# The order of small loads and of sums of squares in a fused attention and expert kernel

## The chip, the cores and the metric

The kernel runs on one core of a Trainium2 chip. The metric is device time in microseconds (us) of one execution. The engines are named as in the profile: PE is TensorE's products, PEld its weight loads, DVE is VectorE, ACT is ScalarE, POOL is GpSimd, SP is SyncE, whose queue issues nearly all loads.

## What is computed

Attention between channels, then a layer of experts on its result, where each token goes to the one expert with the largest logit:

```python
def _attn_ref(q, k, v, tau):                       # B, N, C = 4, 5056, 256
    qn = q / (np.linalg.norm(q, axis=1, keepdims=True) + 1e-06)
    kn = k / (np.linalg.norm(k, axis=1, keepdims=True) + 1e-06)
    s = kn.transpose(0, 2, 1) @ qn / tau
    s = s - s.max(-1, keepdims=True)
    a = np.exp(s)
    a /= a.sum(-1, keepdims=True) + 1e-09
    return v @ a

def _moe_ref(x, w_gate, w1, w2):                   # E, D, F = 8, 256, 1024; x has 20224 rows
    logits = x @ w_gate
    expert_idx = np.argmax(logits, axis=1)
...
    for e in range(E):
        mask = expert_idx == e
        h = np.maximum(x[mask] @ w1[e], 0.0)
        out[mask] = gate_w[mask, None] * (h @ w2[e])
```

The norms of q and k run over the 5056 tokens, so they are sums of squares by channel.

## The kernel before, in words

The four batches of attention run one after the other, and the experts' work begins as soon as the first batch has routed enough tokens. After that three streams share the engines.

*Blocks of tokens.* 72 blocks of 256 tokens and 18 of 128, in six stages; a stage can begin when a batch of attention is done. `block_load` (lines 683 to 695) makes a block's loads on SP: a register is read from the stage's table (line 687), a transposed load brings the rows `xT` (line 692; three buffers, so it waits until the products of three blocks earlier have read theirs), and a small load brings `mt`, 2 KB with each token's factor and row number (line 694; six buffers, so it waits until the store of six blocks earlier has used its own). `block` (from line 697) does 48 products `hp` in four groups (line 720). ACT takes each group out of PSUM as `ht` (line 728, the eviction) and DVE makes its lower half `ht[:, 1]` (line 729). 48 products `y` follow (line 746), two evictions `o` with the token's factor (line 756) and two indirect stores on POOL (line 759). The products' weights `wp` are copied by DVE (line 708).

*Weights.* `weights` (lines 109 to 156) loads an expert's two matrices, 1 MB each (line 116), takes a Gram matrix for a bound on their size (line 132, scale from line 140), and splits them into two halves of 16 bits on ACT (line 150) and DVE (line 151). This fills the first blocks.

*Attention of the next batch.* Products `sp` of keys and queries (line 219), the softmax, products `px` of values (line 389), their copies `xg` and squares (lines 391 and 393), the conversion `rows` (lines 345 and 346) and the scatter to the experts' places in memory (line 516). Pieces of 512 KB called `fed` come through four buffers, with up to three loads ahead (`feed`, line 476). For the norms `by_channel` (lines 171 to 180) has ACT square a piece stored by channel and sum it along the row: 60 instructions at line 178, 54 of them on a `fed` piece. Their sums are needed only once, when all scores of the batch are there.

What sets the order: the Python code writes the three streams interleaved, in portions whose amounts are laid out per stage, and `look` writes a block's loads two blocks ahead. A scheduler then orders each engine's instructions by when it reckons that their inputs are there; a dependency without a semaphore, as the change adds, only says that one instruction stands behind another in the order. On the chip each engine runs its list strictly in that order, and so does SP's queue: an instruction that waits holds everything behind it.

Of the kernel before, what the change touches and what calls it, by code (L numbers as in the profile page):

```python
# [12 lines left out]
F16 = mybir.dt.float16  # L13
BF16 = mybir.dt.bfloat16
I32 = mybir.dt.int32
AF = mybir.ActivationFunctionType
# [4 lines left out]
P = 128  # L21
B, N, C = 4, 5056, 256
# [4 lines left out]
ROW = 258  # L27
# [37 lines left out]
def attention_then_experts(ctx, tc, qk, v, wt, chs, kc, out):  # L65
    nc = tc.nc
    sync, act, vec, pool, pe = nc.sync, nc.scalar, nc.vector, nc.gpsimd, nc.tensor
# [11 lines left out]
    xs = dram.tile([E * NPAD + BLK, ROW], F32, name="xs")  # L79
# [23 lines left out]
    def cell(n):  # L103
        half = place(n // 2)[:, (n % 2) * 2048 : (n % 2 + 1) * 2048]
        return half.bitcast(F32).rearrange("p (j c) -> p j c", j=2)
# [62 lines left out]

    lengths_of = {b: one.tile([P, 4, 5], F32, tag=f"lengths{b % 2}", name="lengths") for b in range(1, B)}

    def by_channel(b):
        lengths = lengths_of[b]
        for n in range(20):
            if b == 1 and n < 6:
                raw = cell(26 + n).rearrange("p j c -> p (j c)")
            else:
                raw = fed("c", b, n).rearrange("p j c -> p (j c)")
            norm = act.activation(raw, raw, AF.Square, accum_out=lengths[:, n // 5, n % 5 : n % 5 + 1])  # L178
            normed.append(norm.ins.name)
            yield 300  # L180

    def split(raw):
# [296 lines left out]
    def fed(*which):  # L479
        if not loading:  # L480
            feed()
        key, raw = loading.pop(0)
        assert key == which, (key, which)
        return raw
# [9 lines left out]
    behind = [None]  # L494
    issued = [None]
    HERE = mybir.DependencyInfo(mybir.DependencyClass.NoSync, mybir.DependencyReason.DATA)

    def after_dma(ins):
        if issued[0] is not None:
            tc.add_manual_dep(ins.ins, issued[0], HERE, reason="stands between two transfers")  # L500
# [35 lines left out]
    def loaded(stage, ins):  # L536
        raw = ins.ins
        if stage < LAST:
            tc.declare_no_dep(raw, group="pads", reason="behind the tokens")
        for s2 in range(stage + 1, LAST):  # L540
            tc.declare_no_dep(raw, group=f"scatter{s2}", reason="blocks read are full already")
        tc.add_to_no_dep_group("loads", raw)
        for name in written[stage] + (written[stage - 1] if stage == LAST else []):
            tc.add_manual_dep(raw, name, SYNC, reason="the stage's rows")
# [10 lines left out]
    def stored(ins):  # L555
        raw = ins.ins
        tc.declare_no_dep(raw, group="stores", reason="a token has one row")
        tc.add_to_no_dep_group("stores", raw)
# [126 lines left out]
    def block_load(stage, tab, i):  # L685
        nt = P if stage == LAST else BLK
        at = nc.values_load(
            tab[1][0:1, i : i + 1], engines=[ENG.SP], min_val=0, max_val=E * NPAD,
            skip_runtime_bounds_check_because=WHY,
        )  # L690
        xT = work.tile([P, 4, BLK], F16, tag="xT", name="xT", bufs=3)[:, :, 0:nt]
        loaded(stage, sync.dma_start_transpose(out=xT, in_=xs[ds(at, nt), 0:C].bitcast(F16)))
        mt = work.tile([P, 2, 2], F32, tag="mt", name="mt", bufs=6)[:, 0 : nt // P, :]
        loaded(stage, sync.dma_start(out=mt, in_=xs[ds(at, nt), C:ROW].rearrange("(j p) c -> p j c", p=P)))
        return xT, mt

    def block(stage, tab, i, xT, mt):
        nt = P if stage == LAST else BLK
        nj = nt // P
        nf = 512 // nt  # L700
        e = nc.values_load(
            tab[0][0:1, i : i + 1], engines=[ENG.DVE], min_val=0, max_val=i if stage == 0 else E - 1,
            skip_runtime_bounds_check_because=WHY,
        )

        def piece(n):
            t = work.tile([P, 1024], F16, tag="wp", name="wp", bufs=WP)
            vec.tensor_copy(out=t, in_=Wf[:, ds(e * 8192 + n * 1024, 1024)])  # L708
            return t

        hts = []
        for f in range(8):
            if f % 2 == 0:
                wp = piece(f // 2).rearrange("p (d s f) -> p d s f", d=2, s=2)
            if f % nf == 0:
                hp = ps_h.tile([P, nf, nt], F32, tag="hp", name="hp")
            n = 0
            for dc in range(2):
                for wh, xh in ((0, 0), (0, 1), (1, 0)):
                    mm = pe.matmul(  # L720
                        hp[:, f % nf, :], wp[:, dc, wh, (f % 2) * P : (f % 2 + 1) * P], xT[:, 2 * xh + dc, :],
                        start=(n == 0), stop=(n == 5),
                    )
                    n += 1
            behind[0] = mm.ins.name
            if f % nf == nf - 1:
                ht = work.tile([P, 2, nf, nt], F16, tag="ht", name="ht", bufs=4)
                act.activation(ht[:, 0], hp, AF.Relu)  # L728
                halved = vec.scalar_tensor_tensor(  # L729
                    out=ht[:, 1], in0=hp, scalar=0.0, in1=ht[:, 0], op0=ALU.max, op1=ALU.subtract  # L730
                )
                hts.append(ht)
            if f % 2 == 1:
                yield
        fac = tiny.tile([P, 2], F32, name="b_fac")[:, 0:nj]
        by = vec.tensor_scalar(out=fac, in0=mt[:, :, 0], scalar1=fe[:, ds(e, 1)], scalar2=None, op0=ALU.mult)
        tc.add_manual_dep(by.ins, halved.ins.name, HERE, reason="the block's rows are here")
        ys = ps_y.tile([P, 2, C], F32, tag="y", name="y")
        wps = []
        for j in range(nj):  # L740
            for n, (hh, wh, f) in enumerate(
                [(0, wh, f) for f in range(8) for wh in range(2)] + [(1, 0, f) for f in range(8)]
            ):
                if j == 0 and n < 16 and n % 4 == 0:
                    wps.append(piece(4 + f // 2).rearrange("p (f s d) -> p f s d", f=2, s=2))
                mm = pe.matmul(  # L746
                    ys[:, j, :], hts[f // nf][:, hh, f % nf, j * P : (j + 1) * P], wps[f // 2][:, f % 2, wh, :],
                    start=(n == 0), stop=(n == 23),
                )
                if (j * 24 + n + 1) % (6 * nj) == 0 and j * 24 + n + 1 < 24 * nj:  # L750
                    behind[0] = mm.ins.name
                    yield
        behind[0] = mm.ins.name
        for j in range(nj):
            o = work.tile([P, C], F32, tag="o", name="o", bufs=2)
            act.activation(o, ys[:, j, :], AF.Copy, scale=fac[:, j : j + 1])  # L756
            gap = pool.memset(idle, 0.0)  # L757
            after_dma(gap)
            ins = pool.indirect_dma_start(  # L759
                out=out[:, :], out_offset=bass.IndirectOffsetOnAxis(ap=mt.bitcast(I32)[:, j, 1:2], axis=0),  # L760
                in_=o, in_offset=None, bounds_check=NT - 1, oob_is_err=False,
            )
            tc.add_manual_dep(ins.ins, gap.ins.name, HERE, reason="behind the pause")
            issued[0] = ins.ins.name
            stored(ins)
        yield
# [46 lines left out]
    rest = work.tile([P, K_N - K_TRI], F32, tag="junk", name="rest", bufs=1)  # L813
# [41 lines left out]
    while len(ahead_of) > G - CUT:  # L855
        fetch()
    norms = by_channel(1)
    take(norms, 6)
    while ahead_of:
# [18 lines left out]
    def look(n, now=True):  # L878
        if n < len(stages) and n not in ahead and stages[n][0] in tables and (now or stages[n][1] > 1):
            ahead[n] = block_load(stages[n][0], tables[stages[n][0]], stages[n][1])  # L880
# [84 lines left out]
    def sides():  # L965
# [3 lines left out]
        yield 0  # L969

    norms_of = {b: by_channel(b) for b in range(2, B)}
    parts = [42 * 1000 + HALF * CHUNK + 10 * 300, 5000 + X_ALL + HALF * CHUNK + 10 * 300]
    parts += [5000 + X_ALL + nch * CHUNK + 20 * 300, 5000 + X_ALL]
# [28 lines left out]
    with tc.If(nc.values_load(  # L1002
        tables[LAST][2][0:1, 0:1], min_val=0, max_val=REST_MOST, skip_runtime_bounds_check_because=WHY
    ) > REST_USUAL):
        more = range(REST_USUAL, REST_MOST)
        loads = {i: block_load(LAST, tables[LAST], i) for i in more}
        for i in more:
            run(block(LAST, tables[LAST], i, *loads[i]))
# [36 lines left out]
```

## Time and profile before

| | |
|---|---|
| median of 3 runs | 1209.59 us (1205.8 to 1214.18) |
| the profiled execution | 1208.84 us, its span in the trace 1207.0 |
| busy: PE, PEld | 1162.8, 1024.9 us |
| busy: DVE, ACT, POOL | 805.6, 619.7, 462.0 us |
| DMA | 177.38 MB, mean 147 GB/s |

The page names for each engine how long it was busy, for groups of instructions what ended the idle time before them, and for stretches of time the granted clock of TensorE and the busy share of the 16 DMA engines. "SPq" is SP's own queue, in which a time is that of issuing a DMA and not of its transfer.

### The profile page before, as it was taken

To read this page: it belongs to the slowest core of one execution; us is meant where nothing else is said; L and a number is where in the kernel's file an instruction comes from. 1 tells how busy PE (TensorE), PEld (TensorE's weight loads), DVE (VectorE), ACT (ScalarE), POOL (GpSimd) and SP (SyncE) were. 2 spreads that over 40 slices of the span, in tenths; PEclk is the share of its full clock that TensorE was granted. 3 is DMA by queue.
4 is the path that set the end of the run, shared out by engine and by line. 5 is a ranking of instruction groups with operands and counts; after the bars stand their busy time and mean duration, and the time that the engine had idled before them with its cause. 6 is when DMAs were issued, how large, how long until landed. Compare 5 with 4: busy or idle time off the path is not lost. (4 is left out here: it accounts for less than half of the span.)

```text
span 1207.0 us, 28339 instructions
## 1 busy us (share of the span) xinstructions
PE 1162.8 (96%) x10194; PEld 1024.9 (85%) x10194; DVE 805.6 (67%) x2122; ACT 619.7 (51%) x1385; POOL 462.0 (38%) x724
## 2 busy tenths in 40 slices
PE   9998899899989999999999999999999999999998
PEld 7777688688878888888888988999878888889997
DVE  5575587767685776666677666767675555556886
ACT  6576377678736665555543555555423333333332
POOL 0066712117771343343345235454462222222222
PEclk9999899999999999999999999999999999999999
DMA  9968989768735555655534232322142122211221
GB/s 377 410 256 291 344 327 269 250 191 244 225 97 146 153 163 159 156 155 163 159 104 104 62 98 84 93 72 75 49 127 53 45 54 54 50 45 45 54 46 26
DMA packets 153488, 177.38 MB, mean 147 GB/s; under 512 B 116604, under 2 KB 118017, under 8 KB 151424
## 3 DMA queue, kind: packets, MB, share of 16 engines
q1 hardware_dynamic: 137952, 133.94, 38.1%
q0 software_dynamic: 15392, 41.60, 9.3%
q8 instruction: 81, 1.33, 0.5%
q14 instruction: 63, 0.52, 0.2%
HBM read 111.49 MB, written 43.29 MB: 128 GB/s over the span
## 5 line engine op out<-in xcount | busy, mean ns | idle before, releaser
L746 PE MATMUL y<-wp,ht 128*128 128x256 f16 x3888 | 457.1, 273 | 15.3 <-ACT ht L728 9.7
L720 PE MATMUL hp<-xT,wp 128*128 128x256 f16 (+1 forms) x4320 | 452.0, 262 | 5.8 <-DVE ht L729 3.8
L746 PEld LDWEIGHTS <-ht 128*128 128x128 f16 x3888 | 372.4, 98 | 71.3 <-ACT ht L728 18.3
L720 PEld LDWEIGHTS <-wp 128*128 128x128 f16 x4320 | 383.0, 98 | 52.1 <-DVE ht L729 4.5
L708 DVE COPY wp<-W 128x1024 f16 (+1 forms) x720 | 291.9, 439 | 181.7 <-PE y L746 138.4
L759 POOL DMA_INDIRECT out<-o,mt x162 | 180.1, 1112 | 480.1 <-ACT o L756 456.8
L728 ACT ACTIVATE ht<-hp 128x512 f16<-128x512 f32 x324 | 191.3, 593 | 160.9 <-PE hp L720 159.0
L729 DVE SCALAR_TENSOR_TENSOR ht<-hp,ht 128x512 f16<-128x512 f32 x324 | 222.3, 687 | 62.6 <-ACT ht L728 61.3
L516 POOL DMA_INDIRECT xs<-rows,r_si x160 | 180.9, 1130 | 141.6 <-ACT rows L345 58.8
L756 ACT ACTIVATE o<-y,b_fac 128x256 f32<-128x256 f32 x162 | 68.9, 468 | 230.8 <-PE y L746 224.5
L506 POOL TENSOR_SCALAR rows<-kt 128x1 int32<-128x1 f32 x160 | 45.5, 284 | 117.2 <-PE sp L219 81.2
L391 ACT COPY xg<-px 128x264 f32<-128x264 f32 x160 | 57.9, 368 | 61.3 <-PE px L389 40.3
L345 ACT ACTIVATE rows<-xg,x_sc 128x256 f16<-128x256 f32 x160 | 71.1, 498 | 25.7 <-issue 8.6
L178 ACT ACTIVATE fed<-fed 128x1024 f32<-128x1024 f32 x54 | 57.0, 1055 | 50.5 <-DMA fed<-in_by_channel 50.4
L346 DVE SCALAR_TENSOR_TENSOR rows<-xg,x_sc,rows 128x256 f16<-128x256 f32 x160 | 71.2, 480 | 15.4 <-ACT rows L345 15.0
L187 DVE TENSOR_TENSOR lo<-fed,hi 128x1024 fp32r<-128x1024 f32 x50 | 61.9, 1239 | 29.1 <-ACT hi L185 29.1
L389 PE MATMUL px<-a_h,hi 128*128 128x264 f32 x240 | 73.3, 308 | 1.5 <-ACT xg L391 0.8
L389 PE MATMUL px<-a_h,lo 128*128 128x264 f32 x240 | 67.3, 287 | 1.2 <-DVE lo L187 1.1
L393 ACT ACTIVATE xjunk<-xg 128x256 bf16<-128x256 f32 x160 | 66.6, 416 | 2.9
L389 PE MATMUL px<-a_l,hi 128*128 128x264 f32 x240 | 67.7, 285 | 0.0
L185 ACT CAST hi<-fed 128x1024 fp32r<-128x1024 f32 x50 | 52.0, 1040 | 17.4 <-DVE c_sf L648 12.3
L389 PEld LDWEIGHTS px<-a_h,hi 128*128 128x128 f32 x240 | 45.2, 189 | 5.8 <-ACT hi L185 2.1
(161 smaller groups left out, 971.5 us busy)
## 6 DMA issues: line engine op xcount, KB each, us to landing
fed<-in_by_channel SPq DMA_DIRECT2D x54, 512.0 KB, 4.3
fed<-in_qk SPq DMA_DIRECT2D x40, 512.0 KB, 4.5
W<-in_w SPq DMA_DIRECT2D x15, 1024.0 KB, 12.9
fed<-in_v SPq DMA_DIRECT2D x30, 512.0 KB, 4.4
raw<-in_qk SPq DMA_DIRECT2D x20, 512.0 KB, 10.1
W<-in_qk SPq DMA_DIRECT2D x20, 512.0 KB, 10.2
W<-in_v SPq DMA_DIRECT2D x10, 512.0 KB, 10.2
W<-in_by_channel SPq DMA_DIRECT2D x6, 512.0 KB
```

Source lines behind the costliest of these rows:

```text
L345: act.activation(r16[:, t, 0:C], x, AF.Copy, scale=by)
L346: vec.scalar_tensor_tensor(out=r16[:, t, C : 2 * C], in0=x, scalar=by, in1=r16[:, t, 0:C], op0=ALU.mult, op1=ALU.subtract)
L389: mm = pe.matmul(px, hl[vh][:, c, ts], ah[:, c, :], start=(n == 0), stop=(n == 5))
L393: act.activation(junk, xg[:, t, 0:C], AF.Square, accum_out=ss[:, h * T + t : h * T + t + 1])
L516: ins = pool.indirect_dma_start(out=xs[:, :], out_offset=bass.IndirectOffsetOnAxis(ap=slot[:n], axis=0), in_=row[:n], in_offset=None)
L708: vec.tensor_copy(out=t, in_=Wf[:, ds(e * 8192 + n * 1024, 1024)])
L720: mm = pe.matmul(hp[:, f % nf, :], wp[:, dc, wh, (f % 2) * P : (f % 2 + 1) * P], xT[:, 2 * xh + dc, :], start=(n == 0), stop=(n == 5),)
L728: act.activation(ht[:, 0], hp, AF.Relu)
L729: halved = vec.scalar_tensor_tensor(out=ht[:, 1], in0=hp, scalar=0.0, in1=ht[:, 0], op0=ALU.max, op1=ALU.subtract)
L746: mm = pe.matmul(ys[:, j, :], hts[f // nf][:, hh, f % nf, j * P : (j + 1) * P], wps[f // 2][:, f % 2, wh, :], start=(n == 0), stop=(n == 23),)
L756: act.activation(o, ys[:, j, :], AF.Copy, scale=fac[:, j : j + 1])
L759: ins = pool.indirect_dma_start(out=out[:, :], out_offset=bass.IndirectOffsetOnAxis(ap=mt.bitcast(I32)[:, j, 1:2], axis=0), in_=o, in_offs ...
```

## The change

A block's small load gets a dependency, for order alone, on its own transposed load. Each square of `by_channel` gets one on the eviction `ht` that was written last before it in the source, whichever block that belongs to. No instruction is added or taken away. Behind the change line numbers are higher: 178 is 184, 692 is 699, 694 is 702, 728 is 738, 756 is 766, 476 is 483.

```diff
@@ -168,6 +168,12 @@
 
     lengths_of = {b: one.tile([P, 4, 5], F32, tag=f"lengths{b % 2}", name="lengths") for b in range(1, B)}
 
+    evicted = []
+
+    def in_turn(ins):
+        if evicted:
+            tc.add_manual_dep(ins.ins, evicted[-1], HERE, reason="behind what the products wait for")
+
     def by_channel(b):
         lengths = lengths_of[b]
         for n in range(20):
@@ -177,6 +183,7 @@
                 raw = fed("c", b, n).rearrange("p j c -> p (j c)")
             norm = act.activation(raw, raw, AF.Square, accum_out=lengths[:, n // 5, n % 5 : n % 5 + 1])
             normed.append(norm.ins.name)
+            in_turn(norm)
             yield 300
 
     def split(raw):
@@ -689,9 +696,12 @@
             skip_runtime_bounds_check_because=WHY,
         )
         xT = work.tile([P, 4, BLK], F16, tag="xT", name="xT", bufs=3)[:, :, 0:nt]
-        loaded(stage, sync.dma_start_transpose(out=xT, in_=xs[ds(at, nt), 0:C].bitcast(F16)))
+        turned = sync.dma_start_transpose(out=xT, in_=xs[ds(at, nt), 0:C].bitcast(F16))
+        loaded(stage, turned)
         mt = work.tile([P, 2, 2], F32, tag="mt", name="mt", bufs=6)[:, 0 : nt // P, :]
-        loaded(stage, sync.dma_start(out=mt, in_=xs[ds(at, nt), C:ROW].rearrange("(j p) c -> p j c", p=P)))
+        rest = sync.dma_start(out=mt, in_=xs[ds(at, nt), C:ROW].rearrange("(j p) c -> p j c", p=P))
+        tc.add_manual_dep(rest.ins, turned.ins.name, HERE, reason="behind its rows")
+        loaded(stage, rest)
         return xT, mt
 
     def block(stage, tab, i, xT, mt):
@@ -725,7 +735,7 @@
             behind[0] = mm.ins.name
             if f % nf == nf - 1:
                 ht = work.tile([P, 2, nf, nt], F16, tag="ht", name="ht", bufs=4)
-                act.activation(ht[:, 0], hp, AF.Relu)
+                evicted.append(act.activation(ht[:, 0], hp, AF.Relu).ins.name)
                 halved = vec.scalar_tensor_tensor(
                     out=ht[:, 1], in0=hp, scalar=0.0, in1=ht[:, 0], op0=ALU.max, op1=ALU.subtract
                 )
```

The first place is ACT in the first block after the first batch of attention. `ht_1252`, `ht_1326`, `ht_1346` and `ht_1372` are the evictions of block 0, `ht_1492` to `ht_1551` three of block 1, `o_1453` and `o_1459` block 0's output; `W_82` with `scales_83` is the split of weights. Before:

```order
L728 ACTIVATE ht_1252<-hp_1239 128x512
L178 ACTIVATE fed_1307,lengths_84<-fed_1307 128x1024
L178 ACTIVATE fed_1309,lengths_84<-fed_1309 128x1024
L728 ACTIVATE ht_1326<-hp_1313 128x512
L150 ACTIVATE W_82<-W_82,scales_83 128x4x256
L728 ACTIVATE ht_1346<-hp_1333 128x512
L150 ACTIVATE W_82<-W_82,scales_83 128x4x256 x2
L728 ACTIVATE ht_1372<-hp_1359 128x512
L150 ACTIVATE W_82<-W_82,scales_83 128x4x256
L756 ACTIVATE o_1453<-y_1379,b_fac_1377 128x256
```

Now, from block 0's second eviction on:

```order
L738 ACTIVATE ht_1326<-hp_1313 128x512
L150 ACTIVATE W_82<-W_82,scales_83 128x4x256
L738 ACTIVATE ht_1346<-hp_1333 128x512
L150 ACTIVATE W_82<-W_82,scales_83 128x4x256 x2
L738 ACTIVATE ht_1372<-hp_1359 128x512
L766 ACTIVATE o_1453<-y_1379,b_fac_1377 128x256
L766 ACTIVATE o_1459<-y_1379,b_fac_1377 128x256
L738 ACTIVATE ht_1492<-hp_1479 128x512
L738 ACTIVATE ht_1529<-hp_1516 128x512
L738 ACTIVATE ht_1551<-hp_1538 128x512
L184 ACTIVATE fed_1307,lengths_84<-fed_1307 128x1024
L184 ACTIVATE fed_1309,lengths_84<-fed_1309 128x1024
```

Both squares have moved from behind block 0's first eviction to behind block 1's third.

The second place is SP's queue in the same stretch: the loads of block 2 (`xT_1498` and `mt_1500`), of an expert's two matrices (`W_82`) and of pieces (`fed`). Before:

```order
L476 DMA fed_1309<-in_by_channel 128x1024
L476 DMA fed_1355<-in_qk 128x1024
L687 TENSOR_LOAD c_tb_815
L694 ISA
L694 DMA mt_1500<-xs_81 128x2x2
L109 TENSOR_LOAD perm_132
L116 ISA
L116 DMA W_82<-in_w 128x2048
L116 ISA
L116 DMA W_82<-in_w 128x2048
L692 ISA
L692 DMA_TRANSPOSE xT_1498<-xs_81 128x4x256
```

Now:

```order
L483 DMA fed_1309<-in_by_channel 128x1024
L483 DMA fed_1355<-in_qk 128x1024
L483 DMA fed_1625<-in_qk 128x1024
L694 TENSOR_LOAD c_tb_815
L699 ISA
L699 DMA_TRANSPOSE xT_1498<-xs_81 128x4x256
L702 ISA
L702 DMA mt_1500<-xs_81 128x2x2
L109 TENSOR_LOAD perm_132
L116 ISA
L116 DMA W_82<-in_w 128x2048
L116 ISA
```

The transposed load has moved ahead of the small load and of the weights, and one piece, `fed_1625`, has moved ahead of all of them.

The third place is ACT some 350 us later: `ht_6481`, `ht_6509` and, behind the copies of attention, `ht_6569` and `ht_6589` are evictions of block 20, `ht_6915` to `ht_6979` are those of block 22. Before:

```order
L728 ACTIVATE ht_6481<-hp_6468 128x512
L728 ACTIVATE ht_6509<-hp_6496 128x512
L178 ACTIVATE fed_6734,lengths_86<-fed_6734 128x1024
L391 COPY xg_6529<-px_6530 128x264
L391 COPY xg_6529<-px_6540 128x264
L393 ACTIVATE xjunk_6538,x_ss_6166<-xg_6529 128x256
L393 ACTIVATE xjunk_6548,x_ss_6166<-xg_6529 128x256
L728 ACTIVATE ht_6569<-hp_6556 128x512
L728 ACTIVATE ht_6589<-hp_6576 128x512
L178 ACTIVATE fed_6827,lengths_86<-fed_6827 128x1024
```

Now, where the two squares stand:

```order
L738 ACTIVATE ht_6787<-hp_6774 128x512
L352 ACTIVATE rows_7407<-xg_6529,x_sc_6167 128x256 x2
L192 CAST hi_6879<-fed_6631 128x1024
L766 ACTIVATE o_6867<-y_6792,b_fac_6790 128x256
L766 ACTIVATE o_6873<-y_6792,b_fac_6790 128x256
L192 CAST hi_7060<-fed_6895 128x1024
L738 ACTIVATE ht_6915<-hp_6902 128x512
L738 ACTIVATE ht_6940<-hp_6927 128x512
L738 ACTIVATE ht_6958<-hp_6945 128x512
L184 ACTIVATE fed_6734,lengths_86<-fed_6734 128x1024
L738 ACTIVATE ht_6979<-hp_6966 128x512
L184 ACTIVATE fed_6827,lengths_86<-fed_6827 128x1024
```

The square of `fed_6734` has moved from behind block 20's second eviction to behind block 22's third, and that of `fed_6827` to behind its fourth.

## Rows read from the trace of the kernel before

**Rows 1.** The page's first part: busy time of each engine, its share, instructions.

```profile
PE 1162.8 (96%) x10194; PEld 1024.9 (85%) x10194; DVE 805.6 (67%) x2122; ACT 619.7 (51%) x1385; POOL 462.0 (38%) x724
```

**Rows 2.** 100-us stretches: length; busy PE, PEld, DVE, ACT, POOL; clock, DMA share, GB/s.

```profile
100.00:200.00 100.00, 94.40 (x751) 80.62 (x749) 73.86 (x208) 65.85 (x128) 46.96 (x75) 0.97 0.90 307
200.00:300.00 100.00, 92.19 (x741) 79.17 (x739) 70.77 (x190) 78.19 (x185) 36.82 (x51) 1.00 0.76 232
```

**Rows 3.** Waits by engine: waiting line, releaser, us in total, times, longest.

```profile
ACT fed L178 <- DMA fed<-in_by_channel: 50.4, 31, 5.1
...
PE y L746 <- ACT ht L728: 9.7, 8, 1.9
```

**Rows 4.** Timeline of ACT, first block: start, us, line, tiles, idle before and releaser.

```profile
133.71 1.06 ACT L178 ACTIVATE fed<-fed 128x1024 f32<-128x1024 f32 x1 [5.09 <-DMA fed<-in_by_channel]
...
136.41 1.06 ACT L178 ACTIVATE fed<-fed 128x1024 f32<-128x1024 f32 x1 [1.55 <-DMA fed<-in_by_channel]
...
137.46 0.58 ACT L728 ACTIVATE ht<-hp 128x512 f16<-128x512 f32 x1
```

**Rows 5.** Timeline of PE in the same stretch.

```profile
138.09 0.61 PE L746 MATMUL y<-wp,ht 128*128 128x256 f16 x4 [1.69 <-ACT ht L728]
139.62 1.03 PE L746 MATMUL y<-wp,ht 128*128 128x256 f16 x4 [0.91 <-ACT ht L728]
142.30 2.32 PE L746 MATMUL y<-wp,ht 128*128 128x256 f16 x10 [1.65 <-ACT ht L728]
```

**Rows 6.** That stretch: all of PE; then line 746 alone, with PEld (columns as rows 2).

```profile
135.80:148.60 12.80, 8.55 (x53) 0.73 1.05 337
...
135.80:148.60 12.80, 7.68 (x48) 5.18 (x47) 0.73 1.05 337
```

**Rows 7.** The chain that ended last, a later block: start, us, what.

```profile
706.72 5.24 PE y L746 x48
```

**Rows 8.** Stretches of 2 us, columns as in rows 2.

```profile
140.00:142.00 2.00, 0.65 (x4) 0.15 (x1) 2.00 (x3) 1.99 (x3) 1.93 (x2) 0.50 1.19 390
...
168.00:170.00 2.00, 2.00 (x36) 1.97 (x33) 2.00 (x5) 2.00 (x5) 1.21 (x1) 1.00 0.11 35
```

**Rows 9.** Timeline of SP's own queue (DMA issues), first block.

```profile
128.64 1.24 SPq L116 DMA_DIRECT2D W<-in_w  x2
136.00 4.44 SPq L692 DMA_TRANSPOSE xT<-xs  x1
```

**Rows 10.** Timeline of PE, 200 to 260 us.

```profile
211.91 1.48 PE L720 MATMUL hp<-xT,wp 128*128 128x256 f16 x12 [1.96 <-DVE ht L729]
...
229.05 1.48 PE L720 MATMUL hp<-xT,wp 128*128 128x256 f16 x12 [0.87 <-DVE ht L729]
...
232.16 2.62 PE L746 MATMUL y<-wp,ht 128*128 128x256 f16 x22 [0.76 <-ACT ht L728]
...
254.74 0.39 PE L389 MATMUL px<-a_h,hi 128*128 128x264 f32 x1 [0.84 <-ACT xg L391]
```

**Rows 11.** Timeline of PE and ACT, 370 to 554 us.

```profile
377.20 1.48 PE L746 MATMUL y<-wp,ht 128*128 128x256 f16 x12 [1.44 <-ACT ht L728]
...
488.83 1.06 ACT L178 ACTIVATE fed<-fed 128x1024 f32<-128x1024 f32 x1 [3.08 <-DMA fed<-in_by_channel]
...
492.01 4.22 PE L746 MATMUL y<-wp,ht 128*128 128x256 f16 x35 [1.94 <-ACT ht L728]
...
519.64 2.31 PE L746 MATMUL y<-wp,ht 128*128 128x256 f16 x18 [0.54 <-ACT ht L728]
...
550.86 2.36 PE L746 MATMUL y<-wp,ht 128*128 128x256 f16 x20 [0.74 <-ACT ht L728]
```

**Rows 12.** Waits of SP's own queue: line, releaser, us in total, times, longest.

```profile
SPq L694 <- DMA out<-o,mt: 383.6, 66, 11.8
...
SPq L692 <- PE hp L720: 67.4, 20, 10.9
...
SPq L476 <- ACT fed L178: 69.6, 37, 11.5
```

## Prediction

> **What bounds the kernel now.** I read the page's engine shares first. TensorE (PE) is busy for 1162.8 of 1207.0 us, the next engine, VectorE (DVE), for 805.6, ScalarE (ACT) for 619.7 [rows 1]. So PE's products set the time, and a change that adds and removes no instruction can win back only part of the 44.2 us in which PE stands idle, and what PE loses while it counts as busy. The windows of 100 us come second: PE is at 94.40 us of 100 in the second and 92.19 in the third, where ACT is at 78.19 [rows 2]. The list of waits comes third. PE waits 9.7 us, 8 times, for the eviction `ht` of line 728 that ACT makes; ACT itself waits 50.4 us, 31 times, for the load of a piece that it is about to square [rows 3]. ACT works in order, so an eviction queued behind such a square waits for that load too. The question is how often that reaches PE, and the timelines answer it stretch by stretch.
>
> **The change part by part: the opening.** In the first block ACT stands idle 5.09 us for one piece, squares it from 133.71, waits 1.55 us for the next, squares that from 136.41, and only at 137.46 starts the eviction that follows [rows 4]. PE, in the same stretch, waits for evictions three times, 1.69, 0.91 and 1.65 us, together 4.25 [rows 5]. That is not all of it. The 48 `y` products of this block lie between 135.80 and 148.60, 12.80 us in which PE is busy 8.55, of which 7.68 are theirs, so 0.87 is other work [rows 6]; in a later block 48 such products take 5.24 [rows 7]. The stretch thus loses 12.80 - 5.24 - 0.87 = 6.7 us. The 2.4 us beyond the idle time have a visible cause: behind the idle time the granted clock is 0.50 from 140 to 142, the lower of its two levels (1.2 GHz), with a mean of 0.73 over the stretch [rows 6, 8].
>
> The Trainium skill (Perfetto Trace Analysis, Identifying the Most-Contended Engine) says that matmul busy time judges poorly how near a kernel is to its limit. Its reading and the idle time differ here, 6.7 against 4.25, and the products' own length decides for the larger.
>
> The change puts both squares behind the second block's third eviction, about one block later, so none of the first block's four evictions has a load to wait for any more. The scale factors of the next expert's weights, which ACT now splits between those evictions, do not hang on these loads. I take the whole 6.7 as removed.
>
> Something comes in exchange on SyncE's queue (SP). Before, two weight loads of 1 MB each are issued at 128.64, ahead of the third block's transposed load, which is issued at 136.00 and takes 4.44 us to issue [rows 9]. Now the block's small load follows its transposed load, and the weights follow both. The transposed load waits for a buffer that the first block's last `hp` product frees, so it can't go much before 136. The weights are issued 136.00 - 128.64 = 7.4 us later at best and 11.8 if the transposed load takes 4.44 again; one load of 512 KB moves up into the gap. DMA runs at 390 GB/s here, and only from 168 to 170 does its share fall to 0.11 [rows 8]. The backlog that ended at 168 will end later, by an estimated 5 us (7.4 to 11.8, less what is still in flight at 128.64 and the load that moved up). Up to about 170 that is hidden by products which have their pieces already; behind it the pieces of keys come late. Bounds: 0, since no row has PE waiting for such a load, to 5.5. I take 1.5, near the zero, for that reason. Opening: -6.7 + 1.5 = -5.2.
>
> **200 to 232 us.** PE waits 1.96, 0.87 and 0.76, sum 3.59, behind evictions that had squares ahead of them on ACT [rows 10]. But ACT has its fullest 100 us here, 78.19 busy [rows 2], no square goes away, and one put behind an eviction stands ahead of the next thing. Bounds: -3.6 to +2.5 (two squares of 1.06, with their read-outs, ahead of something that PE wants). I take a third of the gain, -1.2.
>
> **254 to 554 us.** Single waits on ACT with a square shortly ahead: 0.84 at 254.74 [rows 10], then 1.44, 1.94, 0.54 and 0.74 [rows 11]; sum 5.50. At 488.83 the pattern is plain: ACT waits 3.08 us for a piece, squares it, copies products of attention out, and the eviction that PE waits for until 492.01 stands behind all that [rows 11]. In the new order this square comes some two blocks later, behind an eviction for which its piece has long landed, so this wait goes, and the others likewise. The clock did not fall there, so the idle time is the whole price. What is late next is the operand that DVE prepares. Bounds: all of it to half of it, if in the other half something else of ACT takes the square's place. I take -5.5.
>
> **The later small load.** SP waits 383.6 us, 66 times, at line 694 for a store of six blocks earlier [rows 12]. This sounds like the largest item and is worth nothing by itself: SP computes nothing, and no product waits for the small load, which is used only at the end of the block's first half. Its effect is indirect: loads of pieces stand behind it. Behind the transposed load, the small load's buffer has long been free, and that wait should all but vanish; the pieces are then held by the transposed load, which waits for PE (67.4 us, 20 times, before [rows 12]). One holder replaces another, with the pieces about as early. What hides the difference is the queue of four piece buffers with three loads ahead.
>
> **New waits.** Each square now keeps its buffer longer, up to two blocks. SP already waits 69.6 us, 37 times, for squares to free buffers [rows 12]; that grows, and behind it stand the pieces of keys and values that PE needs. Bounds: 0 (the three loads ahead cover it) to 5 us, a few waits like the ones above. I take +2.
>
> **Sum.** -5.2 - 1.2 - 5.5 + 2.0 = -9.9. The profiled execution took 1208.84 us, 1.8 more than its span, which gives 1198.9; the median of the runs is 0.75 higher and would give 1199.7. I say 1199. From the bounds, the best sum is -6.7 - 3.6 - 5.5 = -15.8 (1193), the worst -1.2 + 2.5 - 2.7 + 5 = +3.6 (1212).
>
> **The rivals.**
>
> All of it comes back: the three loads ahead cover the longer holds and the weights aren't missed. For: no row shows PE waiting for a piece's load. Against: ACT's load in the third 100 us. 1193.
>
> Half of it: ACT's total work is unchanged, so where an eviction moves ahead, the copy of an attention product or the split of a piece falls behind. Then only the opening's idle time, less the late loads (-4.25 + 1.5), and half of the later waits (-2.7) come back, with 1 to 2 us of new ones: -4, 1205. That the change does little at all ends here too; that it does nothing is excluded by the order of instructions, in which the squares do move.
>
> Slower: SP stops at the transposed load, and all loads behind it stop. The rows have this holder 20 times, 3.4 us each on average and 10.9 at most [rows 12]. It decides if a piece that PE needs stands behind it with less than 3.4 us to spare. Place one is the opening, where the weights' 11.8 us come through in full instead of 1.5: -6.7 + 11.8 = +5.1. Place two is the stretch of pieces up to 620 us: five holds that come through at 3.4 make +17, against -6.7 won there. Sum +15, 1224. Against it: the holder stood there before, and no piece was late by it.
>
> On that rival the Trainium skill (DMA: Bandwidth & Descriptors, Anatomy of one DMA) says that DMA engines don't wait on semaphores: any wait happens on the issuing sequencer before dispatch. The trace agrees, as each of these waits is SP's own [rows 12]; by this rule alone every load behind the transposed one would be late by its wait, and the time would be that rival's.
>
> **How the numbers follow.** Forecast (1196 to 1203) 0.37, all of it (1189 to 1196) 0.28, half (1203 to 1212) 0.20, slower (1212 to 1226) 0.15. About 1% is what a measurement of this kernel can tell from no change, here 12.1 us: below 1197.5 counts as faster. That is all of "all" and a third of the forecast's case, 0.28 + 0.12 = 0.40. Slower is what of the last case lies above 1221.7, with a little for what I haven't thought of: 0.12. The rest is 0.48. The range 1190 to 1212 leaves out the last case and a sliver at the bottom, under 0.2.
>
> **What would show it.** In the profile after: the first block's four evictions follow their products at once, PE has no wait for `ht` between 136 and 143, and the clock stays at 1.00 there; ACT's wait for pieces to square falls from 50.4 us to under 20; SP's wait at the small load falls from 383.6 to near nothing, and its wait at the transposed load for `hp` grows; the single waits of 254 to 554 are gone, and PE in the third 100 us is little better than 92.19. Wrong it would be if PE waits for a piece's load, for the split of a piece or for weights behind 165 us, with more than 3 us in sum (the late loads), or if PE idles in the third 100 us as long as before or longer (ACT as the bound there).

## The result and the profile after

The changed kernel takes 1197.95 us (median of 6 runs, 1196.92 to 1198.99) against 1210.38 before (6 runs, 1204.81 to 1214.18). The ratio on record is 0.9909, 95% interval 0.989 to 0.9928; the two medians alone give 0.9897, which lies inside it. The profiled execution has a span of 1196.4 us against 1207.0, so it is 10.6 us shorter.

The engine shares of the page and three of the 100-us windows, which answer to [rows 1, 2]; the last row is the fourth window of the kernel before:

```profile
PE 1162.0 (97%) x10194; PEld 1026.0 (86%) x10194; DVE 807.1 (67%) x2122; ACT 618.4 (52%) x1385; POOL 458.8 (38%) x724
```

```profile
100.00:200.00 100.00, 96.90 (x788) 83.21 (x787) 78.33 (x216) 69.29 (x132) 46.29 (x76) 1.00 0.94 320
200.00:300.00 100.00, 95.13 (x757) 80.92 (x755) 70.62 (x191) 77.41 (x191) 43.71 (x60) 1.00 0.79 237
300.00:400.00 100.00, 92.47 (x745) 80.43 (x746) 71.94 (x216) 58.37 (x151) 47.65 (x78) 0.97 0.49 142
```

```profile
300.00:400.00 100.00, 92.37 (x766) 80.33 (x764) 72.32 (x222) 60.09 (x158) 54.85 (x85) 1.00 0.54 155
```

PE is busy for 0.8 us less than before and idle for 34.4 us instead of 44.2, so the gain is idle time. The second and third 100 us are fuller, by 2.5 and 2.9 us. The fourth has 92.47 busy where before it had 92.37 at a clock of 1.00, and now the clock's mean is 0.97. Something new has come there.

The list of waits, which answers to [rows 3]:

```profile
ACT fed L184 <- DMA fed<-in_by_channel: 13.7, 8, 3.2
...
PEld L756 <- ACT ht L738: 7.2, 28, 1.0
...
PE px L396 <- ACT hi L192: 5.5, 2, 3.2
```

ACT's wait for pieces that it squares has fallen from 50.4 to 13.7 us. Of the waits for the eviction `ht`, only short ones are left: 7.2 us of PE's weight loads, 1.0 at most, and 1.7 us of its products, 0.8 at most (9.7 before). New are two waits for the split of a piece, `hi`.

The waits of SP's own queue, which answer to [rows 12]:

```profile
SPq L699 <- PE hp L730: 332.6, 62, 11.1
SPq L483 <- ACT fed L184: 78.6, 32, 9.2
...
SPq L699 <- PE px L396: 62.1, 10, 10.4
```

The wait at the small load, 383.6 us before, is down to 0.9 in sum and too far down the list to stand here. The wait at the transposed load for `hp` products has grown from 67.4 to 332.6, that for `px` products from 11.5 to 62.1. As time in which SP stands still, the one has replaced the other.

*The opening.* ACT after (columns as in rows 4), then PE (as in rows 5), with one 2-us window of all engines (as in rows 8), then SP (as in rows 9):

```profile
131.91 1.15 ACT L150 ACTIVATE W<-W,scales 128x1024 f16<-128x1024 f32 x1 [3.16 <-DVE scales L87]
132.97 0.58 ACT L738 ACTIVATE ht<-hp 128x512 f16<-128x512 f32 x1
...
134.48 0.58 ACT L738 ACTIVATE ht<-hp 128x512 f16<-128x512 f32 x1
...
137.26 0.58 ACT L738 ACTIVATE ht<-hp 128x512 f16<-128x512 f32 x1
...
149.02 1.05 ACT L184 ACTIVATE fed<-fed 128x1024 f32<-128x1024 f32 x1
```

```profile
135.92 1.47 PE L756 MATMUL y<-wp,ht 128*128 128x256 f16 x12
...
137.40 3.17 PE L226 MATMUL sp<-fed 128*128 128x256 f32 x12
140.40 4.09 PE L756 MATMUL y<-wp,ht 128*128 128x256 f16 x36
...
159.17 3.01 PE L756 MATMUL y<-wp,ht 128*128 128x256 f16 x26 [1.18 <-DVE ht L739]
```

```profile
140.00:142.00 2.00, 2.00 (x18) 1.70 (x17) 1.79 (x11) 0.00 (x0) 1.78 (x3) 1.00 1.09 275
```

```profile
126.04 9.10 SPq L483 DMA_DIRECT2D fed<-in_qk  x2
136.12 1.39 SPq L699 DMA_TRANSPOSE xT<-xs  x1
...
138.95 4.83 SPq L116 DMA_DIRECT2D W<-in_w  x7
```

All four evictions of the first block (132.97 to 137.26, and one earlier) run beside the splits of weights, and the squares come at 149.02. PE goes from block 0's `y` through twelve products of scores and the rest of `y` without a stop, and the clock stays at 1.00 where it was 0.50. PE's own order has changed with it: before, two products of scores stood among block 0's `y`, now twelve do. The transposed load is issued at 136.12 and the weights at 138.95, 10.3 us later than before.

Where the gain was made and lost, by blocks: reading the start of each block's last `y` product from both traces, each counted from its kernel's first `y` product, the changed kernel is ahead by 5.1 us at the end of block 1, 4.2 at block 3, 6.2 at block 5, 8.5 at block 6, 8.2 at block 7, only 2.3 at block 9, 4.3 at blocks 12 to 19, and 10.6 from block 28 on. About 1 us of the 8.5 is not won: eight `px` products of block 6 are done in block 7 now. So 5.9 us are lost between blocks 7 and 9. That is the fourth 100 us. ACT there, then PE, then three windows of PE alone (busy, clock, DMA share, GB/s):

```profile
298.99 1.06 ACT L184 ACTIVATE fed<-fed 128x1024 f32<-128x1024 f32 x1 [3.22 <-DMA fed<-in_by_channel]
...
300.05 0.64 ACT L398 COPY xg<-px 128x264 f32<-128x264 f32 x2
...
300.98 1.04 ACT L192 CAST hi<-fed 128x1024 fp32r<-128x1024 f32 x1
```

```profile
302.08 0.44 PE L396 MATMUL px<-a_h,hi 128*128 128x264 f32 x1 [3.24 <-ACT hi L192]
...
324.81 0.39 PE L396 MATMUL px<-a_h,hi 128*128 128x264 f32 x1 [2.25 <-ACT hi L192]
```

```profile
302.00:304.00 2.00, 1.92 (x9) 0.57 0.61 213
304.00:306.00 2.00, 2.00 (x10) 0.58 0.82 229
306.00:308.00 2.00, 2.00 (x15) 1.00 0.13 41
```

A square waits on ACT until 298.99 for its load. The copies `xg` and the split `hi` stand behind it, and PE waits 3.24 us for the split; then the clock is near a half for four microseconds. The same happens at 324.81, behind which the clock is 0.54 and 0.60 in the windows from 326 to 330.

### The profile page after: what moved, and what is told of

Read it like the earlier page. It is cut to its first block, busy times and chain, and to the rows that moved or that the text cites. A ratio compares the mean times of both kernels' runs of the same rounds, so it can differ in the third digit from the quotient of the medians.

```text
span 1196.4 us, 28325 instructions
## 1 busy us (share of the span) xinstructions
PE 1162.0 (97%) x10194; PEld 1026.0 (86%) x10194; DVE 807.1 (67%) x2122; ACT 618.4 (52%) x1385; POOL 458.8 (38%) x724
## 5 line engine op out<-in xcount | busy, mean ns | idle before, releaser
L730 PEld LDWEIGHTS <-wp 128*128 128x128 f16 x4320 | 383.6, 98 | 46.4 <-issue 2.6
L184 ACT ACTIVATE fed<-fed 128x1024 f32<-128x1024 f32 x54 | 56.7, 1050 | 13.7 <-DMA fed<-in_by_channel 13.7
## 6 DMA issues: line engine op xcount, KB each, us to landing
W<-in_w SPq DMA_DIRECT2D x15, 1024.0 KB, 10.6
```

Of the source, the lines that this page charges most:

```text
L730: mm = pe.matmul(hp[:, f % nf, :], wp[:, dc, wh, (f % 2) * P : (f % 2 + 1) * P], xT[:, 2 * xh + dc, :], start=(n == 0), stop=(n == 5),)
```

## The experiments

All times are medians, with the ratio to the kernel before in the same batch. My theory was that the place of the squares carries the change and that the small load by itself is worth nothing; the rival was that the small load carries it, since loads of pieces queue behind it.

**The squares alone.** The tie of the small load is left out.

```diff
-        tc.add_manual_dep(rest.ins, turned.ins.name, HERE, reason="behind its rows")
```

> Squares behind evictions, the small load free as before. If the place of the squares carries the change (mine): the opening's three waits for ht and the single waits at 254 to 554 us are gone as in the full change, 8 to 11 us under before, about 1200. If the small load carries it, because pieces come earlier once SP no longer stops at it: at most 3 us under before, about 1208. SP's wait at the small load is then some 380 us again under both.

Measured: 1210.95 us against 1211.84, ratio 0.9989 (0.9972 to 1.0007), no difference that can be told from none. That is within what I wrote for the rival and far from my own 8 to 11 us. The opening's wait is gone (4.9 us ahead at the end of block 0, counted as above), and then all of it and more is lost: 2.1 us behind at block 1, 7.9 at block 4. PE, SP and ACT of this kernel, two windows of PE, and SP's wait at the small load between 209 and 219 us:

```profile
156.49 2.93 PE L226 MATMUL sp<-fed 128*128 128x256 f32 x6 [5.37 <-DMA fed<-in_qk]
...
223.62 1.03 PE L755 MATMUL y<-wp,ht 128*128 128x256 f16 x4 [4.59 <-ACT ht L737]
```

```profile
130.25 0.33 SPq L116 DMA_DIRECT2D W<-in_w  x1
137.42 3.40 SPq L699 DMA_TRANSPOSE xT<-xs  x1
141.42 0.89 SPq L116 DMA_DIRECT2D W<-in_w  x2
142.36 0.64 SPq L483 DMA_DIRECT2D fed<-in_qk  x1
...
217.59 0.40 SPq L702 DMA_DIRECT2D mt<-xs  x1
218.08 0.89 SPq L483 DMA_DIRECT2D fed<-in_by_channel  x2
```

```profile
221.93 1.06 ACT L184 ACTIVATE fed<-fed 128x1024 f32<-128x1024 f32 x1 [4.89 <-DMA fed<-in_by_channel]
...
222.99 0.58 ACT L737 ACTIVATE ht<-hp 128x512 f16<-128x512 f32 x1
```

```profile
154.00:156.00 2.00, 0.00 (x0) 0.52 1.05 438
...
158.00:160.00 2.00, 2.00 (x7) 0.50 0.98 410
```

```profile
SPq L702 <- DMA out<-o,mt: 7.7, 1, 7.7
```

At 156.49 PE has waited 5.37 us for a piece of queries and keys. SP issued its load at 142.36, behind weights issued at 130.25 and 141.42 and a transposed load that took 3.40 us; in the full change this piece was issued by 135, ahead of all of them. No wait at a small load is part of that: between 126 and 143 SP waits 6.7 us at the transposed load and not at the small one, so in the opening the tie acts by the order in which SP's loads are put. At 221.93 ACT has waited 4.89 us for a piece to square, whose load was issued at 218.08, right behind a small load that went at 217.59 after SP had waited 7.7 us at it for a store; SP's wait at small loads is 360.7 us again here. This place is the wait of SP that the rival meant. The eviction at 222.99 stands behind this square, and PE waits 4.59 us for it. So a square behind an eviction still blocks the next eviction if its own load is late.

**The small load alone.** The squares are free.

```diff
-            in_turn(norm)
```

> The small load behind its transposed load, the squares free as before. Mine: the two squares of the opening stand ahead of the second eviction again, PE waits some 4 us there and its clock falls, and the time is within 3 us of before, about 1209. If the small load carries the change: 8 us or more under before, about 1201, with ACT's wait for pieces to square well under 50 us.

Measured: 1205.16 us, ratio 0.9943 (0.9923 to 0.9963): 6.7 us under before, more than I allowed and less than the rival asked. The squares do stand ahead of the second eviction again, and ACT waits for pieces nearly as long as before:

```profile
ACT fed L184 <- DMA fed<-in_by_channel: 44.7, 31, 4.4
```

```profile
140.29 0.61 PE L755 MATMUL y<-wp,ht 128*128 128x256 f16 x4 [0.91 <-ACT ht L737]
142.85 1.27 PE L755 MATMUL y<-wp,ht 128*128 128x256 f16 x10 [1.95 <-DVE W L151]
```

```profile
140.00:150.00 10.00, 7.70 (x66) 6.36 (x67) 9.83 (x31) 6.50 (x10) 8.48 (x12) 1.00 1.02 327
```

The opening's waits are there, in other sizes: with an idle time of 0.43 at 138.77 they make 3.29 us, against 4.25 before, and the clock stayed at 1.00 in this execution. At the end of block 0 it is 3.0 us ahead of the kernel before, so about 2 of these are the clock's; whether the small load brings that or the single execution did is not shown. Neither theory is right as it stood: by the ratios the parts give 0.1% and 0.6%, together 0.91% and, in the last batch below, 1.05%.

**The squares also behind the split.**

```diff
+        if cast:
+            tc.add_manual_dep(ins.ins, cast[-1], HERE, reason="behind the split of the piece before it")
...
-        act.copy(out=hi, in_=raw)
+        cast.append(act.copy(out=hi, in_=raw).ins.name)
```

> The full change, and each square also behind the last split of a piece that precedes it in the source. In the changed kernel PE waits 3.24 us at 302 and 2.25 at 325 for such a split, each with the clock at a half behind it, and on ACT a square that waits for its load stands ahead of the split. Mine: that square is the cause, both waits shrink to under 1 us, and the time is 4 to 6 us under the changed kernel, about 1193. Rival: the split's own piece or its buffer is late (a load held at the transposed load), the waits stay, and the time is that of the changed kernel, 1198, within 1.5 us.

Measured: 1191.23 us, ratio 0.9832 (0.9808 to 0.9856), clear of the changed kernel's interval and the fastest of all. By the ratios (0.9909 and 0.9895 for the changed kernel in its two batches) that is 8 to 9 us under the changed kernel, more than the 4 to 6 I expected. ACT near 300 us, its wait for pieces, and two 100-us windows:

```profile
297.61 1.05 ACT L194 CAST hi<-fed 128x1024 fp32r<-128x1024 f32 x1
...
299.88 1.06 ACT L186 ACTIVATE fed<-fed 128x1024 f32<-128x1024 f32 x1 [0.81 <-DMA fed<-in_by_channel]
```

```profile
ACT fed L186 <- DMA fed<-in_by_channel: 7.9, 8, 1.7
```

```profile
200.00:300.00 100.00, 95.98 (x766) 82.30 (x763) 73.50 (x196) 79.82 (x198) 42.64 (x59) 1.00 0.78 241
300.00:400.00 100.00, 95.51 (x809) 84.09 (x808) 75.00 (x222) 60.00 (x154) 50.62 (x81) 1.00 0.53 159
```

The split now runs at 297.61 and the square behind it, still with a wait of 0.81 us for its load, which now holds up nothing that PE needs. The two waits of 3.24 and 2.25 us are gone, the clock is 1.00, and the fourth 100 us has 95.51 us of PE instead of 92.47. Counted by blocks, this kernel is 1.3 us ahead of the changed one at block 7 and 9.5 at block 9, so these two places are worth 8.2. The order on ACT was the cause there and not the split's own piece.

**The tie of the squares in the opening only.**

```diff
-            in_turn(norm)
+            if b == 1 and n < 8:
+                in_turn(norm)
```

> Only the first two squares of the blocks' time are tied behind an eviction, the later 52 are free; the small load as in the change. Mine: the opening's part alone, 4 to 5 us under before, about 1205.5, with the waits at 254 to 554 us back. If the opening's gain is given back later (products only arrive earlier at the next wait): within 2 us of before. If the later squares cost as much as they give: about 1198, as the full change.

Measured: 1203.51 us, ratio 0.9929 (0.9906 to 0.9952), 8.3 us under before. The number is nearest to my case, but I had set it without the 6.7 us that the small load brings alone. The later waits are back, in part:

```profile
228.07 2.19 PE L757 MATMUL y<-wp,ht 128*128 128x256 f16 x18 [1.57 <-ACT ht L739]
```

Against the full change in its two batches (0.9909 and 0.9895) the later squares' tie is worth 0.2 to 0.3%, and the intervals overlap. Against the small load alone (0.9943) the tie of the two opening squares adds 0.14%, and these intervals overlap, too: that the opening's squares win anything on top of the small load is not shown by the times.

After these four I took the theory to be: the squares' place wins only if loads of pieces don't stand behind weights or behind SP's wait at a small load. The next two runs test that, with the changed kernel again beside them.

**The small load tied in the first stage only.**

```diff
-        tc.add_manual_dep(rest.ins, turned.ins.name, HERE, reason="behind its rows")
+        if stage == 0:
+            tc.add_manual_dep(rest.ins, turned.ins.name, HERE, reason="behind its rows")
```

> The full change, but the small load is tied to its transposed load only in the first stage, 5 blocks; from block 5 on it is free. If the small load matters only through the opening (there the tie lets a piece of keys go ahead of the weights): the time of the full change, 1198, within 2 us. If later small loads matter too, because pieces queue behind SP's wait at them: up to the 4.6 us that PE lost at 224 us with the squares alone, and more, so 1203 or above.

Measured: 1206.15 us, ratio 0.9946 (0.9926 to 0.9966). The opening keeps its gain (5.1 us ahead at the end of block 1), and the wait that the squares alone had at 224 is back:

```profile
216.41 1.03 PE L757 MATMUL y<-wp,ht 128*128 128x256 f16 x4 [4.63 <-ACT ht L739]
```

From block 3 to block 4 the kernel falls back by 5.7 us. Just ahead SP waits 8.1 us at the small load that goes at 210.33, and the loads of pieces stand behind it. So later small loads matter too.

**Squares behind eviction and split, small load free.** The third experiment without the tie of the small load.

> Squares behind eviction and split, the small load free everywhere. If the small load's tie is needed for what the squares' place gives (my theory after the first four runs): the opening loses some 7 us again to the piece of keys behind the weights, PE waits some 5 us for it at 156 us, and the time is 1199 or above, against 1191 with the tie. Rival: the tie only helped because squares stood ahead of splits; then 1191 to 1193 without it.

Measured: 1202.94 us, ratio 0.9925 (0.9903 to 0.9946), against 1191.23 with the tie.

```profile
155.42 2.93 PE L228 MATMUL sp<-fed 128*128 128x256 f32 x6 [4.35 <-DMA fed<-in_qk]
...
222.62 1.04 PE L757 MATMUL y<-wp,ht 128*128 128x256 f16 x4 [4.63 <-ACT ht L739]
```

Both waits that the tie had removed are here: the piece behind the weights, and the eviction behind a square whose load came late. The tie is worth 0.9% on top of the best place of the squares. But it is not needed for all that this place gives: without it the time is still 0.75% under the kernel before, where squares behind evictions alone gave nothing (0.9989). So my theory holds for about half of the gain, and the rival's 1191 to 1193 is excluded.

**The change again.**

> The changed kernel itself, on the same chip as the two others: 1198, ratio 0.991 within its interval.

Measured: 1200.14 us, ratio 0.9895 (0.9873 to 0.9916), the same as the first time within the intervals.

## Why the prediction was right, and where it was not

The time was right: 1199 said, 1197.95 measured, and again 1200.14. It was right in part by luck: two terms are wrong by 3.5 to 4 us each, in opposite directions, and cancel.

*The opening.* I took 6.7 us as removed. At the end of block 0 the changed kernel is 4.5 us ahead with ten more products of scores already done, twelve instead of two; eight of these take 1.89 us in the same stretch, so ten are about 2.4, and the sum is 6.9. That the loss was larger than the idle time of 4.25, because of the clock, held. I let 1.5 come back through late weights. By block 3, 4.2 are left, so 2.7 have come back, and most of it not through them: PE's longest stop there, 1.18 us at 159.17, is for DVE, which makes `ht` behind the splits of weights. Weights issued 10.3 us later cost PE nothing that the trace names. The late pieces that I expected behind 165 us came only as 0.48 us at 177.66. A wait of 1.70 at 212.33 is not theirs; it stands under new waits.

*200 to 232 us.* I took -1.2; from block 3 to block 5 the kernel gains 2.0.

*254 to 554 us.* I took -5.5. Block 6 brings 2.2, but 1.3 of it is work done in the blocks beside it (eight `px`, three `hp`), so 0.9 (I had 0.84); block 7 brings 0.6 by the same count, block 12 1.3 (1.44), and blocks 20 to 28 bring 6.2 (the 1.94, 0.54 and 0.74 of my list make 3.2). The single long waits were the right ones, but I left out what is around them. In blocks 20 to 28, 1.2 us is PE's short waits for what DVE makes (0.34, 0.28, 0.39 and 0.23 at 483.63, 522.23, 575.40 and 608.69), which are all gone. The other 1.7 lies in time in which PE counts as busy; there its weight loads still wait for `ht`, 0.15 and 0.28 us at 492.49 and 493.76, for example. The term should have been near 9.

*New waits.* I took +2; it is 5.9 between blocks 7 and 9 alone (8.2 to 2.3). I had written that squares keep buffers longer and that pieces then come late. That is seen once, in PE's 1.70 us at 212.33: the load of this piece goes at 206.94, and between 197 and 208 SP has waited four times for squares:

```profile
SPq L483 <- ACT fed L184: 5.0, 4, 2.6
```

For the 5.9 us my mechanism failed. The trace shows a square that itself waits for its load, with the split of an earlier piece behind it, and the third experiment takes this away by order alone. I had looked for what the squares would be behind, and not for what would be behind the squares.

*The small load.* "Worth nothing by itself" was the wrong step of the prediction. Alone it gives 6.7 us, and without it squares behind evictions give nothing (0.9989); squares behind the splits, too, give 0.75% without it. My argument was that one holder replaces another, and as time of SP that holds (383.6 us gone, 265 more at the transposed load for `hp` and 51 for `px`). But what is behind each holder differs. Before, a piece could stand behind a small load of a later block, which waits for a store; now it stands behind a transposed load alone. The 7.7 us at 217 with the squares alone are such a place; in the opening it is the order of the piece and the weights. That the loads of pieces come early enough for squares and scores is what the fifth and sixth runs show it to be worth. Why this wait for a store falls just ahead of the pieces that matter I have not traced block by block.

*The rival on the slower side*, loads held at the transposed load, did not come: PE's waits for pieces of scores are the 0.48 and 1.70 us above in the profile of the changed kernel. Nor does that holder make the square at 298.99 late: its load goes at 293.35, and the wait at the transposed load just ahead of it is 0.9 us of the 3.2 that the square then waits. The Trainium skill's rule (DMA: Bandwidth & Descriptors, Anatomy of one DMA) that any wait happens on the issuing sequencer before dispatch is in line with the runs: with the squares alone, SP waits 7.7 us at the small load, and the load at 218.08 goes only when this one has gone at 217.59. I had turned the rule against the change, and it speaks for it here, since the wait that held these pieces was the small load's.

Of the two things that I said would show a mistake, one came: PE waits 5.5 us for splits behind 165 us, more than the 3 that I had set. The other did not: PE is less idle in the third 100 us than before (95.13 busy; I had said little better than 92.19).

## What to carry to other kernels

Before an instruction is moved behind another on an engine that works in order, list what will stand behind it in its new place; a filler whose load may be late belongs behind the split that the products need, not only behind the eviction. Two orders that look independent can depend on each other; here one is worth nothing alone and something with the other. Look at which loads stand behind a waiting issue in the queue, not at how long the queue waits. When idle times are added up for an estimate, add the short ones and those of the weight loads, too.

## What the runs showed of the hardware

A stop of PE can cost more than its length. Where PE stood still for 3.24 us the clock was then 0.57 and 0.58 in two windows of 2 us, and the kernel fell back by 4.6 us from block 7 to block 8. In the run with the squares alone, behind 5.37 us of standing still, it was 0.50 to the 160th microsecond, and the kernel fell back by 7 us from block 0 to block 1. It is not so each time: when the changed kernel ran again, a stop of 2.34 us left the clock at 1.00 from 210 to 220, while the one of 2.25 at 324.81 was followed by 0.54 and 0.60.

```profile
215.22 1.99 PE L226 MATMUL sp<-fed 128*128 128x256 f32 x8 [2.34 <-DMA fed<-in_qk]
```

The changed kernel's first `y` product starts at 135.92 us in one profile and at 136.78 in the other, so most of a microsecond between these two executions is of the start alone, and for that reason the blocks were counted from there.
